# Decode attention beside a SwiGLU on one core: value products of 8 tokens by 64 columns, with two heads in one softmax chain

## The chip, the cores and the metric

The kernel runs on one core of one Trainium2 chip. The time is the device time of one execution in microseconds (us). TensorE is called PE in the profile's lines, VectorE DVE, ScalarE ACT, GpSimd POOL and SyncE SP; all bulk loads are issued from SP's queue and carried by the core's 16 DMA engines.

## The reference

One decode step for 4 sequences (B = 4, one query each). The input row x (640 wide) is normalised; from it come a sliding-window attention over cached keys and values and a SwiGLU, and both are added to x.

```python
x = A_x                                   # 4 x 1 x 640, bf16
xn = _layernorm(x, axis=-1)
q = (xn @ wq)                             # 32 heads of 192
k = k_cache[:, :, Sk - W:, :]             # Sk = 8192, W = 2048, 32 heads of 192
v = v_cache[:, :, Sk - W:, :]
p = _softmax(einsum(q, k) * 192 ** -0.5)
attn = einsum(p, v) @ wo                  # wo: 6144 x 640
h = _silu(xn @ w1) * (xn @ w3)            # 1536 wide
return x + attn + h @ w2
```

The keys and values that are read are 32 heads x 4 sequences x 2048 tokens x 192 numbers in bf16, twice: 201 MB. The weights wq, wo, w1, w3 and w2 add 22 MB. Every sequence has its own cache, so a key or a value is used once.

## The kernel before

**Layout.** The window of one head lies in a tile of 128 partitions: a partition holds 64 tokens (NJ) of one sequence, 12288 bf16 numbers, and partition number modulo 4 is the sequence. `load_k` (L98) and `load_v` (L103) each bring one head, 3072 KB, into one of three buffers (KBUFS, VBUFS). `wq` comes first, through the three V buffers; then three K.

**Scores.** A head is cut into 4 chunks of 16 tokens (CH = 16, NC = 4). `mult` (L216) multiplies a chunk of K by the query, which `q_bcast` (L207) has spread over the partitions for two heads at a time: 3072 products a partition on DVE. `adder` (L225) adds them up to 32 numbers a token: six products with the identity, accumulated in PSUM, each of 512 columns. `reduce_tile` (L233) adds those 32 on DVE. `RLAG` makes each reduction stand behind the multiply of two chunks later.

**Softmax chain, one per head.** `chain_lmax` takes the maximum per partition (DVE), `chain_tr` turns it to a row (PE), `chain_gmax` takes the maximum per sequence and spreads it (DVE), `chain_bc` brings it back to the partitions (PE), adds a bias that is -30000 for the three sequences that a partition does not hold (DVE, `negm`), and takes four exponentials, one for each sequence, on ACT (L270). So the weights z come out with three of four columns zero; an ACT instruction also leaves the row sum. `rowsum` (L274) adds these sums over the partitions and takes the reciprocal.

**Value products.** `pv` (L281) multiplies 2 tokens a partition at a time: z gives 32 columns of weights, of which 8 are used, and V 384 columns. Four such products run in the four strips of 32 columns of PE (`g = jj % NG`). 32 products make a head; ACT copies the 128 x 384 result to `o_sb` (L293). `fold` (L297) adds up the strips and the two tokens with two products with `rowsel`, and DVE scales the 4 x 192 result by the reciprocal (L306) into `o_bf`.

**Output.** For each group of four heads `ge_tr` (L308) transposes `o_bf`, and `ge_proj` (L315) multiplies it with that group's part of `wo`, loaded by `wo_load` (L108), into one accumulator for all groups. At the end `ffn_load`, `w2_load`, `ffn_mm` and `ffn_transpose` do the SwiGLU; the last products, with w2 (L420), wait for the last loads. L423 adds the parts and two small DMAs write the result.

**Order.** A table `sched` of slots is written by `add(slot, phase, fn, ...)`: a slot is one chunk, and within a slot the phase orders the calls. The functions are called in that order, and each engine runs its instructions in its own order. Tiles come from pools; a load waits until the last reader of its buffer is done. SP's order of loads is K, V, K, V with `wo` between; towards the end it is K of head 31, V of heads 29 and 30, w1, V of head 31, w3, the last wo and w2 in four pieces.

Of the kernel before, what the change touches and what calls it, by code (L numbers as in the profile page):

```python
# [10 lines left out]
FP32 = mybir.dt.float32  # L11
# [7 lines left out]
def kernel(  # L19
# [12 lines left out]
    DD: int = 32,  # L32
    CH: int = 16,
    HG: int = 4,
    QP: int = 2,
    KBUFS: int = 3,
    VBUFS: int = 3,
    PBUFS: int = 4,
    NZ: int = 3,
    L: int = 9,  # L40
    RLAG: int = 2,
    ALIGN: int = 128,
):

# [16 lines left out]
    NS = H * NC  # L61
    RPP = (HG * Dh) // P
    QW = QP * Dh
    OW = HG * Dh
    NCH = 512
    FC = F // P
    DH = D // 2
    assert NJ % CH == 0 and CH * DD <= 512 and QW <= 512 and CH % 2 == 0
    assert (HG * Dh) % P == 0 and Dh % RPP == 0 and H % HG == 0 and HG % QP == 0
# [3 lines left out]
    NB = H // QP // NG  # L73
    assert H % (QP * NG) == 0 and NB <= 4
    assert DH <= 512 and F % NCH == 0 and NF <= NG and (NJ // 2) % NG == 0 and 2 * B <= 32

# [9 lines left out]
    ps_o = ctx.enter_context(tc.tile_pool(name="ps_o", bufs=2, space=MemoryType.PSUM))  # L86
# [4 lines left out]
    qbcs, wos, o_pss, rss, rcps, o_sbs, o_bfs, chs = ({} for _ in range(8))  # L91
    mult_insts = {}
# [5 lines left out]
    def load_k(h):  # L98
        kt = kpool.tile([P, NJ, Dh], BF16, tag="kt")
        nc.sync.dma_start(out=kt[:], in_=cache_rows(A_k_cache, h))  # L100
        kts[h] = kt

    def load_v(h):  # L103
        vt = vpool.tile([P, NJ, Dh], BF16, tag="vt")
        nc.sync.dma_start(out=vt[:], in_=cache_rows(A_v_cache, h))
        vts[h] = vt
# [6 lines left out]
    x_sb = const.tile([B, D], BF16, name="x_sb")  # L113
# [24 lines left out]
    ones_f = const.tile([P, 1 + ALIGN // 4], FP32, name="ones_f")[:, 0:1]  # L138
    nc.vector.memset(ones_f[:], 1.0)
    nsc = const.tile([1, B], FP32, name="nsc")  # L140
    nc.vector.memset(nsc[:], -SCALE)

    zs = []
    for i in range(NZ):
        z = const.tile([P, NJ // 2, 32], BF16, name=f"z{i}")
        nc.gpsimd.memset(z[:], 0.0)
        zs.append(z)
# [5 lines left out]
    rowsel = const.tile([P, 2 * B], FP32, name="rowsel")  # L153
    nc.vector.tensor_reduce(out=rowsel[:], in_=idf[:].rearrange("p (g c) -> p c g", g=NG)[:, 0:2 * B, :], axis=AX.X, op=ALU.add)
# [9 lines left out]
    sq = ppool.tile([B, D], FP32, tag="pr")  # L164
    ssq = const.tile([B, 1], FP32, name="ssq")
    nc.scalar.activation(out=sq[:], in_=xc[:], func=ACTF.Square, accum_out=ssq[:])
# [6 lines left out]
    xn = const.tile([B, D], BF16, name="xn")  # L173
# [10 lines left out]
    nc.vector.tensor_copy(out=sel[:], in_=rowsel[:, 0:B].unsqueeze(1).to_broadcast([P, NQ, B]))  # L184
    selT = ps_t.tile([P, B], FP32, tag="t")
    nc.tensor.matmul(selT[:], lhsT=sel[0:B].rearrange("k q b -> k (q b)"), rhs=idb[0:B, 0:B], start=True, stop=True)
    mbias = const.tile([P, B], FP32, name="mbias")
    nc.vector.tensor_scalar(out=mbias[:], in0=selT[:], scalar1=-1.0, scalar2=-MASK, op0=ALU.add, op1=ALU.mult)
# [4 lines left out]
    for k in range(NB):  # L193
        pool, tag = ((ps_add, "ps"), (ps_o, "o_ps"))[k // 2]
        qp = pool.tile([P, QW], FP32, tag=tag)
        q_pss.append(qp)
# [7 lines left out]
    for k in range(NB):  # L204
        nc.scalar.copy(out=q_sb[:, k, :], in_=q_pss[k][:])

    def q_bcast(qg):  # L207
        k, g = qg // NG, qg % NG
        bp = ps_t.tile([P, QW], FP32, tag="t")
        nc.tensor.matmul(bp[:], lhsT=sel[32 * g:32 * g + B].rearrange("k q b -> k (q b)"),  # L210
                         rhs=q_sb[32 * g:32 * g + B, k, :], start=True, stop=True)
        qbc = qpool.tile([P, QP, Dh], BF16, tag="qbc")
        nc.scalar.copy(out=qbc[:].rearrange("p h d -> p (h d)"), in_=bp[:])  # L213
        qbcs[qg] = qbc

    def mult(s):  # L216
        h, c = s // NC, s % NC
        pr = ppool.tile([P, CH, Dh], BF16, tag="pr")
        mi = nc.vector.tensor_tensor(out=pr[:], in0=kts[h][:, c * CH:(c + 1) * CH, :],  # L219
                                     in1=qbcs[h // QP][:, h % QP, :].unsqueeze(1).to_broadcast([P, CH, Dh]),  # L220
                                     op=ALU.mult)
        prs[s] = pr
        mult_insts[s] = mi
# [8 lines left out]

    def reduce_tile(s):  # L233
        h, c = s // NC, s % NC
        if c == 0:
            sc = small.tile([P, NJ], FP32, tag="sc", bufs=3)
            scs[h] = sc
        ri = nc.vector.tensor_reduce(out=scs[h][:, c * CH:(c + 1) * CH], in_=pss.pop(s)[:], axis=AX.X, op=ALU.add)  # L238
        ahead = min(s + RLAG, NS - 1)
        if ahead in mult_insts and ahead > s:  # L240
            tc.add_manual_dep(ri.ins, mult_insts[ahead].ins.name, ORDER_DEP, reason="vector engine issue order")

    def chain_lmax(h):
        lmax = small.tile([P, 1], FP32, tag="lmax")
        nc.vector.tensor_reduce(out=lmax[:], in_=scs[h][:], axis=AX.X, op=ALU.max)  # L245
        chs[h] = [lmax]

    def chain_tr(h):
        mt = ps_t.tile([P, P + B], FP32, tag="t")
        nc.tensor.transpose(out=mt[0:1, 0:P], in_=chs[h][0][:], identity=idf[:])  # L250
        chs[h].append(mt)

    def chain_gmax(h):
        gmax = small.tile([1, B], FP32, tag="gmax")
        nc.vector.tensor_reduce(out=gmax[:], in_=chs[h][1][0:1, 0:P].rearrange("o (q b) -> o b q", b=B),
                                axis=AX.X, op=ALU.max)
        gmq = small.tile([1, NQ, B], FP32, tag="gmq", bufs=1)
        nc.vector.tensor_copy(out=gmq[:], in_=gmax[:].unsqueeze(1).to_broadcast([1, NQ, B]))  # L258
        chs[h].append(gmq)

    def chain_bc(h):
        lmax, mt, gmq = chs.pop(h)
        sc = scs.pop(h)
        nc.tensor.matmul(mt[:, P:P + B], lhsT=gmq[:].rearrange("o q b -> o (q b)"), rhs=nsc[:], start=True, stop=True)  # L264
        negm = small.tile([P, B], FP32, tag="negm")
        nc.vector.tensor_tensor(out=negm[:], in0=mt[:, P:P + B], in1=mbias[:], op=ALU.add)  # L266
        z = zs[h % NZ][:].rearrange("p j (s b) -> p j s b", b=B)
        rs = small.tile([P, B], FP32, tag="rs")
        for b in range(B):
            nc.scalar.activation(out=z[:, :, 0:2, b], in_=sc[:].rearrange("p (j s) -> p j s", s=2), func=ACTF.Exp,  # L270
                                 bias=negm[:, b:b + 1], scale=SCALE, accum_out=rs[:, b:b + 1])
        rss[h] = rs

    def rowsum(h):  # L274
        tb = ps_t.tile([B, 1], FP32, tag="t")
        nc.tensor.matmul(tb[:], lhsT=rss.pop(h)[:], rhs=ones_f[:], start=True, stop=True)  # L276
        rcp = small.tile([B, 1], FP32, tag="rcp")
        nc.vector.reciprocal(out=rcp[:], in_=tb[:])  # L278
        rcps[h] = rcp

    def pv(s):  # L281
        h, c = s // NC, s % NC
        if c == 0:
            o_ps = ps_o.tile([P, 2 * Dh], FP32, tag="o_ps")
            o_pss[h] = o_ps
        o_ps, z, vt = o_pss[h], zs[h % NZ], vts[h]
        for jj in range(c * CH // 2, (c + 1) * CH // 2):
            g = jj % NG
            nc.tensor.matmul(o_ps[32 * g:32 * g + 32, :], lhsT=z[:, jj, :], rhs=vt[:, 2 * jj:2 * jj + 2, :],  # L289
                             start=(jj < NG), stop=(jj >= NJ // 2 - NG))  # L290
        if c == NC - 1:
            o_sb = opool.tile([P, 2, Dh], FP32, tag="o_sb")
            nc.scalar.copy(out=o_sb[:].rearrange("r two d -> r (two d)"), in_=o_pss.pop(h)[:])  # L293
            o_sbs[h] = o_sb
            vts.pop(h)

    def fold(h):  # L297
        hg, hl = h // HG, h % HG
        fp = ps_t.tile([B, Dh], FP32, tag="t")
        o_sb = o_sbs.pop(h)  # L300
        for two in range(2):
            nc.tensor.matmul(fp[:], lhsT=rowsel[:, two * B:(two + 1) * B], rhs=o_sb[:, two, :], start=(two == 0), stop=(two == 1))  # L302
        if hl == 0:
            o_bf = opool.tile([B, HG, Dh], BF16, tag="o_bf")
            o_bfs[hg] = o_bf
        nc.vector.tensor_scalar_mul(out=o_bfs[hg][:, hl, :], in0=fp[:], scalar1=rcps.pop(h)[:, 0:1])  # L306

    def ge_tr(hg):  # L308
# [4 lines left out]
        nc.vector.tensor_copy(out=oTs[hg % 2][:, :, 0:B], in_=gp[:])  # L313

    def ge_proj(hg, i):  # L315
        oT = oTs[hg % 2]
        wo_t = wos[hg]
        st = (hg == 0 and i == 0)
# [48 lines left out]
    for h in range(H):  # L367
        s0 = h * NC
        if h >= KBUFS:
            add(s0 - (KBUFS - 1) * NC, 0, load_k, h)  # L370
# [86 lines left out]
```

## Time and profile before

| | |
|---|---|
| median of 3 runs | 529.87 us |
| lowest and highest run | 528.54 and 530.36 us |
| the profiled execution: time, span | 528.51 us, 526.6 us |
| mean granted clock of TensorE | 0.853 |
| busy: PE, DVE, ACT, POOL | 360.0, 340.2, 76.4, 4.5 us |
| moved by the DMA engines | 223.33 MB, mean 424 GB/s |

The span runs from the first to the last instruction of the profiled execution, and 1.9 us of its time lie outside it. Busy times are sums over instructions; a profile cuts the span in 40 slices of 13.2 us and gives, for each, tenths of busy time by engine and the rate of the DMA engines. "Issue to landing" of a load is the time from its DMA instruction on SP to its completion, with the time that it stands behind others.

### The profile page before, as it was taken

Reading aid. Unit: us, or ns where it says so; the run is one execution under the profiler, and the core shown is the slowest. Engines: PE = TensorE matmul, PEld = TensorE weight load, DVE = VectorE, ACT = ScalarE, POOL = GpSimd, SP = SyncE. Lnnn points to the kernel's source line nnn. Section 1 sums busy time; section 2 is a strip of 40 time slices with the busy share of each in tenths; the row PEclk is TensorE's granted clock in tenths of the full one; section 3 lists DMA queues with packets and bytes.
Section 4 is the critical chain, followed back from the end, with each engine's and each line's share of the span. In section 5 each row is a group of like instructions: output and inputs, shape, how many; then the busy total and the mean of one; then the engine's idle time right before and its main releaser. Section 6 shows DMA issues by size and latency. Waiting matters only on the chain.

```text
span 526.6 us, 5872 instructions
## 1 busy us (share of the span) xinstructions
PE 360.0 (68%) x2384; PEld 148.4 (28%) x2384; DVE 340.2 (65%) x475; ACT 76.4 (15%) x318; POOL 4.5 (1%) x14
## 2 busy tenths in 40 slices
PE   1356767886676778767567976767678766668755
PEld 1122222332222333232222322223233322223322
DVE  4069766677666557777556677666567775665802
ACT  2101211101111111101111011111111011111130
POOL 3000000000000000000000000000000000000000
PEclk9999988778788887887878787888887887888888
DMA  8999999999999999999999999999999999999995
GB/s 359 439 425 437 429 429 431 432 424 435 437 429 435 429 434 429 433 432 431 429 433 428 426 440 426 437 429 431 432 433 431 429 436 430 431 426 440 423 426 218
DMA packets 11730, 223.33 MB, mean 424 GB/s; under 512 B 1316, under 2 KB 1464, under 8 KB 2872
## 3 DMA queue, kind: packets, MB, share of 16 engines
q1 hardware_dynamic: 11688, 222.97, 98.7%
q8 instruction: 18, 0.29, 0.2%
q14 instruction: 8, 0.07, 0.0%
q10 hardware_dynamic: 16, 0.01, 0.0%
HBM read 222.96 MB, written 0.01 MB: 423 GB/s over the span
## 4 chain that ended last, share of the span: by engine, by line
DMA 66%; DVE 21%; PE 9%; ACT 2%; issue 2%; SPq 0%; DVEq 0%; ACTq 0%
DMA kt<-in_A_k_cache_dram 61%; DVE pr L219 15%; PE ps L229 6%; DMA w2t<-in_B_w_dram 5%; DVE sc L238 5%; PE o_ps L289 1%; ACT z L270 1%; PE acc L321 1%; ACT o_sb L293 0%; DVE lmax L245 0%; SPq L129 0%; PE gp L312 0%; PE tb L276 0%; DVE rcp L278 0%; SPq L335 0%
## 5 line engine op out<-in xcount | busy, mean ns | idle before, releaser
L229 PE MATMUL ps<-pr,idb 128*128 128x512 bf16 x768 | 241.0, 470 | 110.4 <-DVE sc L238 101.1
L219 DVE TENSOR_TENSOR pr<-kt,qbc 128x3072 bf16<-128x3072 bf16 x128 | 223.3, 1745 | 35.5 <-DMA kt<-in_A_k_cache_dram 35.4
L229 PEld LDWEIGHTS <-idb 128*128 128x128 bf16 x768 | 85.3, 115 | 240.0 <-issue 190.4
L238 DVE TENSOR_REDUCE sc<-ps 128x16 f32<-128x512 f32 x128 | 86.9, 679 | 0.9 <-PE ps L229 0.9
L293 ACT COPY o_sb<-o_ps 128x384 f32<-128x384 f32 x32 | 15.1, 472 | 306.5 <-PE o_ps L289 306.5
L289 PE MATMUL o_ps<-vt,z 128*32 128x384 bf16 x1024 | 55.3, 334 | 3.8 <-DMA vt<-in_A_v_cache_dram 3.8
L270 ACT ACTIVATE z<-sc,negm 128x64 bf16<-128x64 f32 x128 | 45.7, 423 | 76.7 <-DVE negm L266 76.7
L266 DVE TENSOR_TENSOR negm<-mt,mbias 128x4 f32<-128x4 f32 x32 | 5.2, 161 | 70.7 <-PE mt L264 70.7
L306 DVE TENSOR_SCALAR o_bf<-fp,rcp 4x192 bf16<-4x192 f32 x32 | 12.9, 405 | 56.8 <-PE fp L302 29.9
L302 PE MATMUL fp<-o_sb,rowsel 128*4 128x192 f32 x128 | 26.7, 332 | 13.2 <-ACT o_sb L293 13.2
L289 PEld LDWEIGHTS <-z 128*32 128x32 bf16 x1024 | 25.0, 97 | 29.4 <-issue 20.8
L270 ACT ACTIVATION_READ_ACCUMULATOR z<-sc,negm 128x1 f32 x128 | 23.9, 187 | 0.0
L302 PEld LDWEIGHTS fp<-o_sb,rowsel 128*4 128x4 f32 x128 | 8.7, 87 | 24.2 <-ACT o_sb L293 18.6
L276 PE MATMUL tb<-ones_f,rs 128*4 128x1 f32 x64 | 6.2, 166 | 13.4 <-ACT z L270 13.4
L264 PE MATMUL mt<-nsc,gmq 1*128 1x4 f32 x64 | 12.2, 258 | 1.2 <-DVE gmq L258 1.2
L264 PEld LDWEIGHTS mt<-nsc,gmq 1*128 1x128 f32 x64 | 9.4, 183 | 12.1 <-issue 10.3
L276 PEld LDWEIGHTS tb<-ones_f,rs 128*4 128x4 f32 x64 | 3.6, 86 | 24.5 <-ACT z L270 23.0
L278 DVE RECIPROCAL rcp<-tb 4x1 f32<-4x1 f32 x32 | 4.9, 153 | 8.5 <-PE tb L276 8.5
L201 PE MATMUL qp<-wt,xnT 128*32 128x384 bf16 x80 | 7.0, 523 | 4.9 <-DMA wt<-in_A_wq_dram 4.9
L250 PE MATMUL mt<-idf,lmax 128*1 128x128 f32 x32 | 9.9, 308 | 0.5 <-DVE lmax L245 0.4
L321 PE MATMUL acc<-wt,oT 128*32 128x320 bf16 x96 | 9.7, 301 | 0.3 <-DVE oT L313 0.2
L213 ACT CAST qbc<-bp 128x384 bf16<-128x384 f32 x16 | 7.6, 485 | 7.7 <-PE bp L210 7.7
(61 smaller groups left out, 80.1 us busy)
## 6 DMA issues: line engine op xcount, KB each, us to landing
kt<-in_A_k_cache_dram SPq DMA_DIRECT2D x32, 3072.0 KB, 36.8
vt<-in_A_v_cache_dram SPq DMA_DIRECT2D x32, 3072.0 KB, 40.1
wt<-in_A_wo_dram SPq DMA_DIRECT2D x8, 960.0 KB, 36.5
wt<-in_A_wq_dram SPq DMA_DIRECT2D x2, 3072.0 KB, 13.2
wt<-in_B_w_dram SPq DMA_DIRECT2D x2, 1920.0 KB, 32.5
wt<-in_A_wq_dram SPq DMA_DIRECT2D x1, 1536.0 KB
w2t<-in_B_w_dram SPq DMA_DIRECT2D x2, 640.0 KB, 26.9
w2t<-in_B_w_dram SPq DMA_DIRECT2D x1, 480.0 KB, 27.6
```

The costliest lines, as they stand in the source:

```text
L219: mi = nc.vector.tensor_tensor(out=pr[:], in0=kts[h][:, c * CH:(c + 1) * CH, :], in1=qbcs[h // QP][:, h % QP, :].unsqueeze(1).to_broadcast ...
L229: nc.tensor.matmul(ps[:], lhsT=idb[:], rhs=pr[:, :, kk * DD:(kk + 1) * DD], start=(kk == 0), stop=(kk == NK - 1))
L238: ri = nc.vector.tensor_reduce(out=scs[h][:, c * CH:(c + 1) * CH], in_=pss.pop(s)[:], axis=AX.X, op=ALU.add)
L250: nc.tensor.transpose(out=mt[0:1, 0:P], in_=chs[h][0][:], identity=idf[:])
L264: nc.tensor.matmul(mt[:, P:P + B], lhsT=gmq[:].rearrange("o q b -> o (q b)"), rhs=nsc[:], start=True, stop=True)
L270: nc.scalar.activation(out=z[:, :, 0:2, b], in_=sc[:].rearrange("p (j s) -> p j s", s=2), func=ACTF.Exp, bias=negm[:, b:b + 1], scale=SCAL ...
L276: nc.tensor.matmul(tb[:], lhsT=rss.pop(h)[:], rhs=ones_f[:], start=True, stop=True)
L289: nc.tensor.matmul(o_ps[32 * g:32 * g + 32, :], lhsT=z[:, jj, :], rhs=vt[:, 2 * jj:2 * jj + 2, :], start=(jj < NG), stop=(jj >= NJ // 2 - NG))
L293: nc.scalar.copy(out=o_sb[:].rearrange("r two d -> r (two d)"), in_=o_pss.pop(h)[:])
L302: nc.tensor.matmul(fp[:], lhsT=rowsel[:, two * B:(two + 1) * B], rhs=o_sb[:, two, :], start=(two == 0), stop=(two == 1))
L306: nc.vector.tensor_scalar_mul(out=o_bfs[hg][:, hl, :], in0=fp[:], scalar1=rcps.pop(h)[:, 0:1])
L321: nc.tensor.matmul(acc[32 * t:32 * t + 32, :], lhsT=oT[:, i, :], rhs=wo_t[:, i * D + t * DH:i * D + (t + 1) * DH], start=st, stop=sp)
```

## The change

The kernel is cut in other pieces; the loads and the sums stay the same.

- The chunk doubles: CH = 32, NC = 2. `mult` handles 6144 products, `adder` takes twelve products that leave 16 numbers a token (DD = 16), and `reduce_tile` adds those. There are two `pr` buffers of twice the size for four. Queries are spread for eight heads at a time, in three pieces of 512 columns.
- Two heads (HH = 2, a pair u) share one softmax chain: one maximum step, one transpose, one `negm`, one reciprocal for both. The exponential is taken once for each head, without the bias, and `chain_z` multiplies it on DVE by a mask `selb` that is one for the partition's own sequence: z for both heads at once.
- `pv` takes 8 tokens and 64 columns of the head at a time: 32 columns of weights, all used, and 512 columns of V; the three thirds of the head's 192 columns run in three strips. 24 products make a head, in one slot. Only the part of the result where weight and value are of the same token counts: `pick` multiplies by a mask `diag`, `pick_sum` adds over the tokens, both on DVE and both for two heads at once, except in the last pair, where each head has its own. `fold` brings the strips together for two heads, and the scaling by the reciprocal goes to ACT (L344 after).
- Small DVE steps are tied behind the multiply of the slot in which they are called (`behind`), one chunk later than what they use.
- There is one PSUM buffer `o_ps` of two heads for two of one head. Some tiles share buffers, and the masks are made from the identity at the start.

The diff, cut to its core:

```diff
-    DD: int = 32,
-    CH: int = 16,
+    DD: int = 16,
+    CH: int = 32,
     HG: int = 4,
-    QP: int = 2,
+    QP: int = 8,
     KBUFS: int = 3,
     VBUFS: int = 3,
-    PBUFS: int = 4,
-    NZ: int = 3,
-    L: int = 9,
-    RLAG: int = 2,
-    ALIGN: int = 128,
+    PBUFS: int = 2,
+    L: int = 7,
+    ALIGN: int = 144,
...
+    slot = [0]
+
+    def behind(inst):
+        if slot[0] in mult_insts:
+            tc.add_manual_dep(inst.ins, mult_insts[slot[0]].ins.name, ORDER_DEP, reason="vector engine issue order")
+
     def reduce_tile(s):
...
-        ahead = min(s + RLAG, NS - 1)
-        if ahead in mult_insts and ahead > s:
-            tc.add_manual_dep(ri.ins, mult_insts[ahead].ins.name, ORDER_DEP, reason="vector engine issue order")
+        behind(ri)
...
-        for b in range(B):
-            nc.scalar.activation(out=z[:, :, 0:2, b], in_=sc[:].rearrange("p (j s) -> p j s", s=2), func=ACTF.Exp,
-                                 bias=negm[:, b:b + 1], scale=SCALE, accum_out=rs[:, b:b + 1])
+        for hh in range(HH):
+            nc.scalar.activation(out=e[:, hh, :], in_=sc[:, hh, :], func=ACTF.Exp,
+                                 bias=negm[:, hh:hh + 1], scale=SCALE, accum_out=rs[:, hh:hh + 1])
...
+    def chain_z(u):
+        e = es.pop(u)
+        z = small.tile([P, HH, NJ, B], BF16, tag="z", bufs=2)
+        behind(nc.vector.tensor_tensor(out=z[:].rearrange("p h j b -> p (h j) b"),
+                                in0=e[:].rearrange("p h j -> p (h j)").unsqueeze(2).to_broadcast([P, HH * NJ, B]),
+                                in1=selb[:].unsqueeze(1).to_broadcast([P, HH * NJ, B]), op=ALU.mult))
+        zts[u] = z
...
-        for jj in range(c * CH // 2, (c + 1) * CH // 2):
-            g = jj % NG
-            nc.tensor.matmul(o_ps[32 * g:32 * g + 32, :], lhsT=z[:, jj, :], rhs=vt[:, 2 * jj:2 * jj + 2, :],
-                             start=(jj < NG), stop=(jj >= NJ // 2 - NG))
-        if c == NC - 1:
-            o_sb = opool.tile([P, 2, Dh], FP32, tag="o_sb")
-            nc.scalar.copy(out=o_sb[:].rearrange("r two d -> r (two d)"), in_=o_pss.pop(h)[:])
...
+        GN = NJ // PL
+        for g in range(GN):
+            for k in range(NV):
+                nc.tensor.matmul(o_ps[32 * k:32 * k + 32, hh, :],
+                                 lhsT=z[:, hh, g * PL:(g + 1) * PL, :].rearrange("p l b -> p (l b)"),
+                                 rhs=vt[:, g * PL:(g + 1) * PL, k * DV:(k + 1) * DV],
+                                 start=(g == 0), stop=(g == GN - 1))
+
+    def pick(u, h0, h1):
...
+        n = (h1 - h0) * PL
+        behind(nc.vector.tensor_tensor(out=o_ms[u][:, h0:h1].rearrange("r h l d -> r (h l) d"),
+                                       in0=o_pss[u][0:NV * 32, h0:h1, :].rearrange("r h (l d) -> r (h l) d", l=PL),
+                                       in1=diag[0:NV * 32, h0:h1, :].rearrange("r h l -> r (h l)").unsqueeze(2).to_broadcast([NV * 32, n, DV]), op=ALU.mult))
+
+    def pick_sum(u, h0, h1):
...
+        behind(nc.vector.tensor_reduce(out=o_rs[u][:, h0:h1, :], in_=o_ms[u][:, h0:h1].rearrange("r h l d -> r h d l"), axis=AX.X, op=ALU.add))
...
-        for two in range(2):
-            nc.tensor.matmul(fp[:], lhsT=rowsel[:, two * B:(two + 1) * B], rhs=o_sb[:, two, :], start=(two == 0), stop=(two == 1))
...
-        nc.vector.tensor_scalar_mul(out=o_bfs[hg][:, hl, :], in0=fp[:], scalar1=rcps.pop(h)[:, 0:1])
+        for k in range(NV):
+            nc.tensor.matmul(fp[:, :, k * DV:(k + 1) * DV], lhsT=fsel[0:NV * 32, k, :], rhs=o_r[:], start=True, stop=True)
...
+        for hh in range(HH):
+            nc.scalar.mul(out=o_bfs[hg][:, pr + hh, :], in_=fp[:, hh, :], mul=rcp[:, hh:hh + 1])
...
+    PS = HH * NC
+    for j in range(H):
+        if j >= KBUFS:
+            add(NC * j - 3, 0, load_k, j)
+        add(NC * j + 2, 8, load_v, j)
+        add(NC * j + L, 2, pv, j)
+    for s in range(NS):
+        add(s, 1, mult, s)
+        add(s, 3, adder, s)
+        add(s + 1, 4, reduce_tile, s)
+    for u in range(H // HH):
+        e = u * PS + PS - 1
+        add(e + 1, 5, chain_lmax, u)
+        add(e + 2, 2, chain_tr, u)
+        add(e + 2, 5, chain_gmax, u)
+        add(e + 3, 2, chain_bc, u)
+        add(e + 3, 5, chain_z, u)
+        add(e + 4, 2, rowsum, u)
...
+        add(PS * u + NC + L + 3, 2, fold, u)
...
-    add(end + L - NC, 0, ffn_mm, 1)
-    add(end + L + 1, 7, ffn_mm, 3)
-    add(end + L + 3, 7, ffn_transpose)
+    add(end + 4, 0, ffn_mm, 1)
+    add(end + 9, 0, ffn_mm, 3)
+    add(end + 10, 0, ffn_transpose)
```

## The prediction

> **What bounds the kernel now.** I read the page first: the span, the slices of the DMA engines, the queues.
>
> ```profile
> span 526.6 us, 5872 instructions
> ...
> DMA  8999999999999999999999999999999999999995
> GB/s 359 439 425 437 429 429 431 432 424 435 437 429 435 429 434 429 433 432 431 429 433 428 426 440 426 437 429 431 432 433 431 429 436 430 431 426 440 423 426 218
> ...
> q1 hardware_dynamic: 11688, 222.97, 98.7%
> q8 instruction: 18, 0.29, 0.2%
> ```
>
> The 16 DMA engines are busy in every slice but the first and the last, and 38 slices in a row move 423 to 440 GB/s. A slice is 13.17 us; the 223.33 MB less the 359 and 218 GB/s of the two end slices make 215.7 MB in 500.3 us, 431 GB/s. No compute engine comes near: PE 68%, DVE 65%, ACT 15%. So the span is the start, the stream of 223 MB, and what follows the last byte. The chain on the page names vector and matrix steps for a third of the span, but only because the issue of a K load waits for a multiply to free its buffer. Whether that issue is early or late is told by the answers for the tiles `kt` and `vt`:
>
> ```profile
> L100 SPq DMA_DIRECT2D kt<-in_A_k_cache_dram x32: 534/535/674, 2.1 to 449.1; - x32
> ...
> DMA to landing us min/median/max: 34.8/36.8/41.3
> ```
>
> ```profile
> L105 SPq DMA_DIRECT2D vt<-in_A_v_cache_dram x32: 534/535/596, 13.8 to 483.2; - x32
> ...
> DMA to landing us min/median/max: 29.8/40.1/43.2
> ```
>
> One load is 3.146 MB, 7.3 us at 431 GB/s. It lands 37 to 40 us after its issue, so four others stand ahead of it and some 30 us of compute delay are free in every head. Third, the end, by windows of 1 us (PEclk is the figure after PE to POOL, then the DMA share and GB/s):
>
> ```profile
> 510.00:511.00 1.00, 0.00 (x0) 0.00 (x0) 0.00 (x0) 0.00 (x0) 0.00 (x0) 1.00 1.08 464
> ...
> 513.00:514.00 1.00, 1.00 (x19) 0.55 (x12) 0.00 (x0) 0.00 (x0) 0.00 (x0) 0.50 1.01 428
> ...
> 516.00:517.00 1.00, 0.50 (x10) 0.47 (x12) 0.43 (x2) 0.00 (x0) 0.00 (x0) 1.00 1.05 437
> ...
> 520.00:521.00 1.00, 1.00 (x17) 0.67 (x13) 0.43 (x2) 0.00 (x0) 0.00 (x0) 1.00 0.56 229
> ...
> 522.00:523.00 1.00, 0.56 (x10) 0.29 (x6) 0.00 (x0) 0.00 (x0) 0.00 (x0) 1.00 0.10 40
> ```
>
> The stream thins out from 519 us: some of the 16 engines finish up to 4 us before the slowest. And fourth, the timeline from the landing of the last V:
>
> ```profile
> 511.86 2.75 PE L289 MATMUL o_ps<-vt,z 128*32 128x384 bf16 x32 [3.81 <-DMA vt<-in_A_v_cache_dram]
> ...
> 514.65 0.48 ACT L293 COPY o_sb<-o_ps 128x384 f32<-128x384 f32 x1 [5.32 <-PE o_ps L289]
> ...
> 515.19 0.81 PE L302 MATMUL fp<-o_sb,rowsel 128*4 128x192 f32 x4 [0.58 <-ACT o_sb L293]
> ...
> 516.87 1.26 PE L342 MATMUL gt<-wt,xnT 128*32 128x512 bf16 x15
> ...
> 518.79 0.42 DVE L353 TENSOR_TENSOR hb<-sg,t_bf 96x512 bf16<-96x512 bf16 x1 [1.64 <-ACT t_bf L346]
> ...
> 519.55 0.99 PE L321 MATMUL acc<-wt,oT 128*32 128x320 bf16 x12
> ...
> 520.38 0.71 PE L420 MATMUL ff<-w2t,hT 128*32 128x320 bf16 x8
> 521.75 0.72 PE L420 MATMUL ff<-w2t,hT 128*32 128x320 bf16 x8 [0.66 <-DMA w2t<-in_B_w_dram]
> 522.91 0.72 PE L420 MATMUL ff<-w2t,hT 128*32 128x320 bf16 x8 [0.44 <-DMA w2t<-in_B_w_dram]
> 523.67 0.48 DVE L423 TENSOR_TENSOR res<-ff,t 64x320 bf16<-64x320 f32 x1 [2.25 <-PE ff L420]
> ```
>
> The last eight products of w2 wait for data until 522.91; everything before them waits less. That is the wait that ends last. The attention tail has a small margin to it.
>
> **The change, part by part.** *The stream.* Same loads, sizes, queue and three buffers each. On SP only a wo load changes places with a neighbouring K or V load, which costs nothing as long as all are issued early. Engine traffic does not slow the stream: 428 GB/s between 30 and 60 us with DVE 91% busy, 427 between 480 and 500 with 64%. Cost 0.
>
> *The lead of the loads.* DVE's small steps now stand behind a multiply that waits for K, and the values of a head are multiplied in the second half-chunk slot three heads later, so V buffers come free later. Let K of head j land at T; heads follow at 2 x 7.3 = 14.6 us. Two multiplies: I price one of 6144 elements from L219 (1745 ns for 3072) and L353 (422 ns for 512), which give 0.517 ns an element: 3.34 us (at most 2 x 1.745 = 3.49). PE sums 24 products a head as before, some 1.4 us for six (the chain's `PE ps` rows), 2.9 us a chunk. With the mask multiply and the value products ahead of the second chunk, V's buffer of head j-3 or j-2 is free 9 to 11 us after a K landing, and queued behind it on SP is a K load. The issue of a V then falls from 40 us ahead of its landing to about 51 - 25 = 26 us (four heads' K and V between them); K goes from 37 to about 33. A V needs 7.3. Cost 0, covered by some 18 us in each head; were that cover gone, each us missing would be paid up to 29 times.
>
> *DVE, for two heads.* Out: 8 multiplies x 1.745 + 8 reductions x 0.679 + 2 x (0.208 + 0.269 + 0.214 + 0.161 + 0.153 + 0.405) = 22.2 us. In: 4 x 3.34 + 4 x 0.68 + one chain of five steps, 1.1 + the mask multiply z + `pick` and `pick_sum` on 1024 f32 elements. L423 (320 f32 from PSUM, 483 ns) and L238 (512, 679 ns) give 1.02 ns an element, so 1.20 each. z is 512 bf16: 0.42 by L353, 0.68 by L238; its first operand is repeated with step 0, which no row shows, so I take 0.68. Sum 20.2 us: DVE falls by about 2 us in every 29.2, some 32 us of 340, all beside the stream: worth 0. The Trainium skill ("VectorE: DVE Perf Modes", section "Mode 2×_1P") asks step 1 of every 16-bit operand for the double rate, which speaks against z; by it z keeps the dearer price, which no row here shows, and the sum stays.
>
> *PE and ACT.* Value products: 32 of 384 columns in four strips become 24 of 512 in three, 8 rounds of 512 columns for 8 of 384, a third longer: about +0.6 us a head. ACT loses six of eight exponentials a pair with their accumulator reads (0.423 + 0.187) and two copies (0.472), and gains two scalings. All hidden; PE is idle for 5 us in a head (32% of the span over 32 heads).
>
> *The start.* DVE builds more masks and three query broadcasts precede the first multiply instead of two; ACT's six copies of 384 columns at 0.49 become six of 512 at 0.58 (L346's 512), +0.6 us, while the first K lands only at 30.3. Cost 0.
>
> *The tail.* From 511.86, where V of the last head lands, in after's order on PE: value products, fold, w3's products, transposes, output projection, w2's products. Value products: three strips, like L342, whose five rounds of 512 took 2.19 us at a granted 0.50 (504.59) and 1.26 at 1.00 (516.87). Eight rounds are 3.50 or 2.02; the clock there is 0.50, so they end at 515.4 (before: 514.6). `pick` and `pick_sum` on 512 elements, 0.68 + 0.05 to pass the semaphore, twice: 516.85. Fold: 3 x 128 columns for two heads is what 2 x 192 were, 0.81: 517.7. ACT scales two heads, 0.8 (two of the 0.42 us row): 518.5. Beside that PE runs w3's products, 1.26: 519.0; cast 0.58, product 0.42, transposes 0.36 and gaps: 520.5, and only then, in PE's order, the projection, 0.99: 521.5. Three eights of w2 at 0.72: 523.66, against 522.91 + 0.74 = 523.65 before. So the margin is used up exactly; cost 0.0. If the value products got the full clock it is -1.5 us of slack and still 0; if the two new DVE steps and two scalings each cost 0.2 more, +0.8; if PE is granted half again after its gap, more (first rival).
>
> *Instruction words.* Fewer instructions on PE: 3696 rows in its order for 4322. The 18 fetches (16 KB each) should become about 15 or 16. Spread over all DMA engines two or three less are worth 0.1 us; on the slowest engine alone, at 431/16 = 27 GB/s, 0.6 us each, 1.8. I take 0.1.
>
> Sum: 526.6 - 0.1 + 0.1 (half a chance of a late tail) = 526.6 us of span, 528.5 with the 1.9 around it (528.51 for that execution). The median of the runs, 529.87, lies 1.4 above that execution; I forecast 529.8.
>
> **The rivals.** *Slower, the clock in the tail (and a tail longer than counted).* The change puts 1.45 us of DVE between the value products and the fold, on a PE that had 0.50 from 512 to 515 after idling from 509. If half is granted from about 518, the projection and w2's products take 1.74 times as long (2.19/1.26): 0.74 x (0.99 + 2.16) = +2.3 us, 532.2. It decides as soon as the projection ends after 521.5. The Trainium skill ("TensorE: Matmul & The Clock Gate", section "Part 1: The HAM clock gate") holds that only an idle window of about 3.4 us brings half the clock; the idle 508.6 to 511.8 before the 0.50 fits, and by it the gap of 1.45 us would cost nothing. Chance 0.16, with the same end reached by dearer steps.
>
> *Slower, the queue runs dry.* V issues come later than 29 us after the landing they follow. At 1 us a head that is +29, 559 us. Against it stands the 18 us of cover. 0.04.
>
> *Faster, the slowest DMA engine has less to do.* The thinning from 519 to 523 is 16 engines ending apart; three fetches less on the last of them take 1.8 us, 528.0 by the median. For it: everything after V's landing shifts along. Against: nothing shows which engine carries the fetches. 0.13.
>
> *No change that can be told,* the forecast: 0.67.
>
> **How the numbers follow.** A measurement of this kernel tells about 0.3%, 1.6 us, from no change. Likeliest 529.8; the fetches at their bound give 528.0, the tail at half the clock 532.2, and the runs before spread by 0.9 around their middle. Range 527.9 to 532.1, outside it the dry queue and the outermost of both ends. Faster 0.13, same 0.67, slower 0.20.
>
> **What would show it.** Right: DMA still 9 in all middle slices near 431 GB/s; V landing 24 to 29 us after issue and K 31 to 35; DVE near 308 us, a multiply at 3.34, z at 0.4 to 0.7, `pick` of both heads at 1.2; the last products of w2 still waiting for DMA, or starting within 0.3 us of it; the projection ending near 1.4 us before the last w2 byte. Wrong: a slice under 420 GB/s in the middle (dry queue), the last chain running V, `pick`, fold, projection without a DMA wait behind it (tail), or a stream that ends over 1.5 us earlier (fetches).

## The result, and the profile after

| after | |
|---|---|
| median of 6 runs | 526.94 us (526.79 to 527.74) |
| median of 6 runs of before beside it | 529.61 us (528.51 to 531.14) |
| the profiled execution: time, span | 526.79 us, 525.0 us |
| mean granted clock of TensorE | 0.844 |
| busy: PE, DVE, ACT, POOL | 326.4, 328.3, 39.6, 1.8 us |

After takes 0.9955 of the time of before, with a 95% interval of 0.9936 to 0.9974. Of the 2.7 us between the medians, 1.7 (0.3%) are in the two profiled executions. The rest depends on which runs of before are in the comparison: its 101 runs in the four later comparisons fall in two groups, 72 between 528.05 and 529.1 us and 29 from 529.2 to 531.4, and four of the six here lie in the upper one. After's six runs and the 22 of e4, f1 and e5 below, which are after with small edits, lie closer: 22 of the 28 between 526.79 and 527.16, six between 527.6 and 527.91. In the later comparisons, where before's median is 528.4 to 528.6, the gain is about 1.5 us.

The stream did not change. The page of after, with the slices of the DMA engines and the queues:

```profile
span 525.0 us, 4658 instructions
...
GB/s 360 433 436 428 431 436 426 438 426 433 431 432 432 433 434 427 436 429 429 439 424 434 429 435 426 438 422 439 434 430 429 430 434 434 430 433 430 426 428 256
...
q1 hardware_dynamic: 11688, 222.97, 99.0%
q8 instruction: 15, 0.25, 0.2%
```

Every slice between the first and the last still moves 422 to 439 GB/s, and q1 carries the same packets and bytes. What is smaller is q8, the instruction words: 15 fetches for 18. The answers for the tiles `kt` and `vt` of after, a load's issue and its time to landing:

```profile
L107 SPq DMA_DIRECT2D kt<-in_A_k_cache_dram x32: 534/550/687, 2.1 to 447.4; - x32
...
DMA to landing us min/median/max: 30.7/34.3/41.1
```

```profile
L112 SPq DMA_DIRECT2D vt<-in_A_v_cache_dram x32: 534/535/595, 13.4 to 493.6; - x32
...
DMA to landing us min/median/max: 25.6/32.4/38.4
```

A V load now lands 32.4 us after its issue, 40.1 before, and one load needs 7.3 us: the lead is still four loads deep. The page's costliest groups (busy us, mean ns of one, idle time before them and its releaser) hold the vector engine's terms (the 17 of L331 and of L323 are 15 for two heads, 1912 and 1209 ns each, and two for one head):

```profile
L228 DVE TENSOR_TENSOR pr<-kt,qbc 128x6144 bf16<-128x6144 bf16 x64 | 214.5, 3352 | 166.8 <-DMA kt<-in_A_k_cache_dram 166.8
...
L331 DVE TENSOR_REDUCE o_r<-o_m 96x128 f32<-96x1024 f32 (+1 forms) x17 | 30.7, 1807 | 0.1
...
L323 DVE TENSOR_TENSOR o_m<-o_ps,diag 96x1024 f32<-96x1024 f32 (+1 forms) x17 | 19.5, 1148 | 7.6 <-PE o_ps L313 7.6
...
L291 DVE TENSOR_TENSOR z<-e,selb 128x512 bf16<-128x512 bf16 x16 | 10.8, 678 | 0.9 <-ACT e L283 0.9
```

DVE now waits 166.8 us for K: it is not the bound. Then the end, the timeline from the landing of the last V (start, length, what; in brackets the wait before it):

```profile
510.43 1.91 PE L313 MATMUL o_ps<-vt,z 128*32 128x512 bf16 x24 [0.62 <-DMA vt<-in_A_v_cache_dram]
...
512.39 0.69 DVE L323 TENSOR_TENSOR o_m<-o_ps,diag 96x512 f32<-96x512 f32 x1 [2.51 <-PE o_ps L313]
513.11 1.01 DVE L331 TENSOR_REDUCE o_r<-o_m 96x64 f32<-96x512 f32 x1
...
517.57 0.99 PE L357 MATMUL acc<-wt,oT 128*32 128x320 bf16 x12
...
518.63 0.72 PE L467 MATMUL ft<-w2t,hT 128*32 128x320 bf16 x8
...
520.17 0.72 PE L467 MATMUL ft<-w2t,hT 128*32 128x320 bf16 x8 [0.81 <-DMA w2t<-in_B_w_dram]
...
521.31 0.72 PE L467 MATMUL ft<-w2t,hT 128*32 128x320 bf16 x8 [0.42 <-DMA w2t<-in_B_w_dram]
...
522.07 0.48 DVE L470 TENSOR_TENSOR res<-ft,attn_bf 64x320 bf16<-64x320 f32 x1 [2.63 <-PE ft L467]
```

The same wait ends last, the last eight products of w2 for their load, but at 521.31 instead of 522.91: 1.60 us, the whole difference of the spans. The last V, too, landed 1.43 us sooner (510.43 for 511.86). So the stream itself ended earlier, at the same rate and with the same bytes. The windows of 1 us of after show what is missing (PEclk after POOL, then DMA share and GB/s):

```profile
521.00:522.00 1.00, 0.69 (x8) 0.41 (x7) 0.00 (x0) 0.00 (x0) 0.00 (x0) 1.00 0.13 47
522.00:523.00 1.00, 0.03 (x2) 0.00 (x0) 0.48 (x1) 0.00 (x0) 0.00 (x0) 1.00 0.00 0
```

In before the DMA engines still had a share of 0.10 between 522 and 523: in the trace's packet records two of the 16 engines end there, at 522.8 and 523.0, while six end near 521.3, one at 521.87 and the other seven sooner. In after the latest seven end between 521.1 and 521.4, and nobody behind them.

### The profile page after: what moved, and what is told of

Same layout as the page of the kernel before. It is cut to its first block, busy times and chain, and to the rows that moved or that the text cites. A ratio compares the mean times of both kernels' runs of the same rounds, so it can differ in the third digit from the quotient of the medians.

```text
span 525.0 us, 4658 instructions
## 1 busy us (share of the span) xinstructions
PE 326.4 (62%) x1991; PEld 142.2 (27%) x1991; DVE 328.3 (63%) x289; ACT 39.6 (8%) x121; POOL 1.8 (0%) x11
## 4 chain that ended last, share of the span: by engine, by line
DMA 77%; DVE 13%; PE 8%; SPq 1%; issue 0%; DVEq 0%
DMA kt<-in_A_k_cache_dram 73%; DVE pr L228 11%; PE ps L238 6%; DMA w2t<-in_B_w_dram 5%; PE o_ps L313 1%; DVE sc L253 1%; SPq L112 0%; DVE o_r L331 0%; SPq L136 0%; DVE o_m L323 0%; PE acc L357 0%; SPq L372 0%; PE ft L467 0%; DVE z L291 0%; DVE res L470 0%
## 5 line engine op out<-in xcount | busy, mean ns | idle before, releaser
L238 PE MATMUL ps<-pr,idb 128*128 128x512 bf16 x768 | 223.7, 452 | 166.3 <-DVE pr L228 166.3
L228 DVE TENSOR_TENSOR pr<-kt,qbc 128x6144 bf16<-128x6144 bf16 x64 | 214.5, 3352 | 166.8 <-DMA kt<-in_A_k_cache_dram 166.8
L313 PE MATMUL o_ps<-vt,z 128*32 128x512 bf16 x768 | 66.3, 389 | 1.2 <-DMA vt<-in_A_v_cache_dram 0.6
L253 DVE TENSOR_REDUCE sc<-ps 128x32 f32<-128x512 f32 x64 | 43.7, 683 | 6.8 <-PE ps L238 6.7
L331 DVE TENSOR_REDUCE o_r<-o_m 96x128 f32<-96x1024 f32 (+1 forms) x17 | 30.7, 1807 | 0.1
L283 ACT ACTIVATE e<-sc,negm 128x64 bf16<-128x64 f32 x32 | 10.9, 340 | 239.4 <-DVE negm L279 239.4
L323 DVE TENSOR_TENSOR o_m<-o_ps,diag 96x1024 f32<-96x1024 f32 (+1 forms) x17 | 19.5, 1148 | 7.6 <-PE o_ps L313 7.6
L344 ACT ACTIVATE o_bf<-fp,rcp 4x192 bf16<-4x192 f32 x32 | 11.4, 403 | 132.0 <-PE fp L338 132.0
L338 PE MATMUL fp<-o_r,fsel 96*4 96x128 f32 x96 | 13.1, 273 | 1.8 <-DVE o_r L331 1.8
L291 DVE TENSOR_TENSOR z<-e,selb 128x512 bf16<-128x512 bf16 x16 | 10.8, 678 | 0.9 <-ACT e L283 0.9
## 6 DMA issues: line engine op xcount, KB each, us to landing
kt<-in_A_k_cache_dram SPq DMA_DIRECT2D x32, 3072.0 KB, 34.3
vt<-in_A_v_cache_dram SPq DMA_DIRECT2D x32, 3072.0 KB, 32.4
```

The lines of the kernel that those rows point to most:

```text
L228: mi = nc.vector.tensor_tensor(out=pr[:], in0=kts[j][:, c * CH:(c + 1) * CH, :], in1=qbcs[j // QP][:, j % QP, :].unsqueeze(1).to_broadcast ...
L238: nc.tensor.matmul(ps[:], lhsT=idb[:], rhs=pr[:, :, kk * DD:(kk + 1) * DD], start=(kk == 0), stop=(kk == NK - 1))
L253: ri = nc.vector.tensor_reduce(out=scs[j // HH][:, j % HH, c * CH:(c + 1) * CH], in_=pss.pop(s)[:], axis=AX.X, op=ALU.add)
L283: nc.scalar.activation(out=e[:, hh, :], in_=sc[:, hh, :], func=ACTF.Exp, bias=negm[:, hh:hh + 1], scale=SCALE, accum_out=rs[:, hh:hh + 1])
L291: behind(nc.vector.tensor_tensor(out=z[:].rearrange("p h j b -> p (h j) b"), in0=e[:].rearrange("p h j -> p (h j)").unsqueeze(2).to_broadc ...
L313: nc.tensor.matmul(o_ps[32 * k:32 * k + 32, hh, :], lhsT=z[:, hh, g * PL:(g + 1) * PL, :].rearrange("p l b -> p (l b)"), rhs=vt[:, g * PL: ...
```

## Experiments

The theory: the two late engines of before are those that carried one more of q8's fetches, so the time goes by how many instructions PE has. The main rival: other buffer addresses, or something else in the new order, sped up the stream. In all tables *fetches* are q8's, *V31* is the start in us of the last head's value products, which begin when V lands, and the ratio is to the runs of before beside it.

**Instructions put back.** The kernel after, with n tiny products in every slot, into columns of `acc`'s bank that nothing reads (e1 six, e2 sixteen, f1 two, f2 four, f3 twenty), 128 instructions for each step of n:

```diff
+    def extra(n):
+        for _ in range(n):
+            nc.tensor.matmul(acc_full[64:96, 320:324], lhsT=idb[:, 0:32], rhs=idb[:, 0:4], start=True, stop=True)
...
+        add(s, 3, extra, 6)
```

e1: 

> The changed kernel with 6 more tiny products (32 columns of weights, 4 of data, into a part of PSUM that nobody reads) in each of the 64 slots: 768 more PE instructions, 4464 rows in PE's order for 3696, nothing else changed. Fetch theory (the end is set by the slowest DMA engine, which also carries PE's instruction words): 18 fetches of 16 KB as in the kernel before, and the time goes back up by 0.6 us (fetches spread over several engines) to 1.8 us (three on the slowest, 16 KB at 27 GB/s each): 527.6 to 528.8. Rival (the gain comes from the order of the loads, the place of the buffers or the tail): 526.9, no change, since PE has over 2 us free in a slot of 7.3.

e2: 

> As the run with 6 more tiny products, with 16 in each slot: 2048 more PE instructions, 5744 rows, some 8 more fetches than the changed kernel, 23 in all. Fetch theory: 3 times the shift of the smaller dose, +1.6 to +4.9 us, 528.5 to 531.8. Rival: 526.9; at most a little more if the 1.2 us of PE time in each slot were to reach the path.

f1: 

> The changed kernel with 2 more tiny PE products in each slot: 256 instructions, 3952 rows, 16 fetches. Staircase theory (PE's fetches go round in turn over 8 of the 16 DMA engines, each costs its engine about 1.4 us, and the engine with the most sets the end, so the time goes by the number of fetches over 8, rounded up: 15 and 16 give 2, 17 to 24 give 3): 526.9, as the changed kernel. Proportional theory (each fetch adds its share): +0.3 to +0.6, 527.2 to 527.5.

f2: 

> The same with 4 in each slot: 512 instructions, 4208 rows, 17 fetches. Staircase theory: one engine now has a third, 528.3 to 528.4 as with 18 and with 23; of the last microsecond of the stream, 522 to 523, about one engine in 16 is busy. Proportional theory: 527.4 to 527.9.

f3: 

> The same with 20 in each slot: 2560 instructions, 6256 rows, 25 fetches. Staircase theory: a fourth on one engine, 1.4 us over the runs with 18 and 23, 529.8. Saturation theory (something else holds the end at 528.4, and the tiny products only bring that back): 528.4.

**Sums left out.** Fewer instructions, in before and in after, by ending `adder`'s loop early: e3 is before with 3 of 6 sums, g1 before with 4 of 6, e5 after with 6 of 12.

```diff
-        for kk in range(NK):
+        for kk in range(NK // 2):
...
-                             start=(kk == 0), stop=(kk == NK - 1))
+                             start=(kk == 0), stop=(kk == NK // 2 - 1))
```

e3: 

> The kernel before with three of the six sums of a chunk left out (the scores are those of half the head's width, so the output is another): 768 PE instructions fewer, 3554 rows for 4322, 15 fetches for 18; every load, the order and the place of the buffers and DVE's work stay. Fetch theory: faster than the kernel before by as much as the change is, 527.0 (by 0.6 to 1.8 us at least). Rival (order, place or tail of the changed kernel): 529.6, no change.

e5: 

> The changed kernel with six of the twelve sums of a chunk left out (scores of half the head's width, so the output is another): 768 PE instructions fewer, 2928 rows, 12 fetches for 15. Staircase theory: still 2 on the fullest engine, 526.9, and some of the seven engines that end last now end earlier; proportional theory: 525.4 to 526.5. If PE, less busy, is granted half its clock at the end, the tail adds up to 2 us to either, which the timeline shows as last products that wait for no load.

g1: 

> The kernel before with two of the six sums of a chunk left out (scores of two thirds of the head's width, so the output is another): 512 PE instructions fewer, 3810 rows for 4322, 16 fetches for 18, everything else as it was. Staircase theory: no engine has a third fetch, and the old kernel runs at 527.0, as the changed one; the window 522 to 523 shows no transfer. Rival (the change's other parts are needed too): 528.5, as before. If PE, less busy, is granted half its clock at the end, the tail hides part of it, as where half of the sums were left out.

**As few as possible.** g3 is after with 2 of 12 sums and 5 of 8 steps of the value products, and ten filler products ahead of the tail.

g3: 

> The changed kernel with ten of the twelve sums and three of every eight steps of the value products left out (the output is another), and ten filler products near the end that keep PE at work: 1860 rows, 8 fetches. Staircase theory: one fetch on each engine, 1.4 us under the changed kernel, 525.5, the lowest step but one; the stream's last microsecond is 519 to 520. Saturation theory (15 fetches and fewer no longer matter): 526.9. A PE at half its clock would add up to 2 us, which the timeline shows as last products without a wait for a load.

| kernel | fetches | V31 | median us (range) | ratio (95%) |
|---|---|---|---|---|
| g3 | 8 | 509.06 | 526.43 (525.65 to 527.96) | 0.9948 (0.9929 to 0.9967) |
| e5 | 12 | 510.46 | 527.06 (526.92 to 527.70) | 0.9974 (0.9963 to 0.9985) |
| after | 15 | 510.43 | 526.94 (526.79 to 527.74) | 0.9955 (0.9936 to 0.9974) |
| e3 | 15 | 510.77 | 528.26 (527.37 to 530.41) | 0.9999 (0.9984 to 1.0013) |
| f1 | 16 | 510.90 | 527.03 (526.89 to 527.91) | 0.9967 (0.9951 to 0.9983) |
| g1 | 16 | 510.77 | 527.98 (527.16 to 529.99) | 0.9985 (0.9970 to 1.0000) |
| f2 | 17 | 512.08 | 528.27 (527.95 to 529.22) | 0.9991 (0.9979 to 1.0003) |
| e1 | 18 | 512.06 | 528.41 (528.10 to 529.08) | 0.9994 (0.9985 to 1.0003) |
| before | 18 | 511.86 | 528.4 to 528.6 in four comparisons | 1 |
| e2 | 23 | 511.77 | 528.45 (528.34 to 529.23) | 0.9995 (0.9983 to 1.0006) |
| f3 | 25 | 513.04 | 529.61 (529.38 to 530.53) | 1.0014 (1.0004 to 1.0025) |

The column V31 is a staircase: 509.1 with 8 fetches, 510.4 to 510.9 with 12 to 16, 511.8 to 512.1 with 17 to 23, 513.0 with 25. Its steps lie between 8 and 12, at 16 to 17, and between 23 and 25; they are 1 to 1.4 us high. That is the form of fetches dealt in turn to eight engines: the fullest engine has one, two, three or four, and the last bytes of a load wait for the fullest. e2 first contradicted the theory as I had it: sixteen products a slot were to cost about three times what six cost, and cost the same. f1, f2 and f3 were then chosen to have the fetch counts 16, 17 and 25 at the edges of a staircase, and fell on it. The DMA share between 522 and 523 us counts the engines that have one more. The windows of e2 (23 fetches) and of f2 (17), then of f3 (25) one microsecond later:

```profile
522.00:523.00 1.00, 0.55 (x10) 0.30 (x6) 0.00 (x0) 0.00 (x0) 0.00 (x0) 1.00 0.34 129
```

```profile
522.00:523.00 1.00, 1.00 (x10) 0.57 (x8) 0.48 (x2) 0.00 (x0) 0.00 (x0) 0.50 0.07 26
```

```profile
523.00:524.00 1.00, 0.63 (x8) 0.35 (x8) 0.00 (x0) 0.00 (x0) 0.00 (x0) 1.00 0.06 24
```

0.34 of 16 engines is five or six busy throughout; in e2's packet records seven engines end between 522.7 and 523.0. 0.07 is one engine, and in f2 one ends at 523.0, the seventeenth fetch. 0.06 is again one, f3's twenty-fifth, at 524.1. So a single one of the 16 engines sets the time, and one fetch makes the step. In each of these runs as many engines end last as the fetches leave over when divided by eight: two in before (18 fetches), four in e5 (12), seven in after (15) and e2 (23), one in f2 and f3.

The packet records show the deal and the price of a fetch directly. The 18 fetches of before take, in order, 947, 879, 880, 934, 938, 925, 962, 962 ns, then 956, 884, 880, 935, 929, 922, 967, 962, then 954 and 879: a row of eight durations that comes round again, within 9 ns. And the 24 KB packet that begins as a fetch ends takes 1380 to 1462 ns in after, where most take 912. Fetch and lengthened packet together hold up the engine by 1.42 to 1.43 us, in 14 of after's 15 fetches; behind the last one comes no such packet. That is the step's height.

The runs of e3 and g1 show a second thing. Both end their stream with the lower step (V31 at 510.77, no DMA after 522), yet e3's median did not move. Each has two groups of runs: six of e3's twelve and six of g1's lie between 527.16 and 527.68, below all 101 runs of before (528.05 and more), and the others from 528.29 up. So half of the runs show the step, about 1 us; the 0.4 to 0.5 us that they still lie above after are not explained. The timelines of g1 and of e3:

```profile
521.90 0.72 PE L420 MATMUL ff<-w2t,hT 128*32 128x320 bf16 x8 [0.45 <-DMA w2t<-in_B_w_dram]
```

```profile
521.88 3.41 PE L420 MATMUL ff<-w2t,hT 128*32 128x320 bf16 x24
...
525.33 0.48 DVE L423 TENSOR_TENSOR res<-ff,t 64x320 bf16<-64x320 f32 x1 [2.37 <-PE ff L420]
```

In g1's profiled execution (527.36 us) the last eight wait for the load. In e3's (530.03 us, one of the longer of its runs) all 24 w2 products start only at 521.88, when the load is there, and take 3.41 us at a granted clock of 0.50 where three eights take 2.16 at 1.00: the tail has become the bound and gives back what the fetches gave. f2's profiled execution, 529.22 us and the longest of its runs, has the same: its stream ends at 523.0, but its 24 products take 3.03 us from 521.43 at 0.50. With 3 of 6 sums left out PE idles more (mean granted clock 0.668). g3 shows it too: its stream is earliest, but its 24 w2 products take 3.02 us from 518.51, at half the clock until 521, without a wait for DMA; only its best runs, 525.65 and 525.69, reach the next step down.

**Places of the buffers.** `ALIGN` is the size of an unused tile that moves the K and V buffers; with it they start at an odd multiple of 256 bytes in after, and at a multiple of 512 in before. e4 sets 400 for 144 (a multiple of 512 again), h3 sets 112 (32 bytes below a multiple of 256).

e4: 

> The changed kernel with ALIGN = 400 for 144, which shifts every later tile in SBUF by 256 bytes, so that the K, V and wo buffers start at multiples of 512 bytes as in the kernel before (in the changed one at odd multiples of 256). Place theory: the gain of 2.7 us goes, or part of it. Fetch theory: 526.9, no change.

e4: 526.95 us (526.79 to 527.66), ratio 0.9971 (0.9960 to 0.9982). Where the tiles lie modulo 512 does nothing, and f2 and e1, whose extra products leave the loads and the buffers where after has them, lose the gain: the rivals of the addresses and of the order are out for this change.

**Instructions on ACT.** g2 adds eight tiny copies a slot on ACT, 512 in all; h2 is g2 with `ALIGN` 112, because g2's small tile had also moved the buffers by 32 bytes.

g2: 

> The changed kernel with 8 tiny ACT copies (4 numbers a partition) behind each multiply: 512 more ACT instructions, four more fetches of 8 KB, PE as it is. If every engine's fetches go round the same eight DMA engines as PE's: one or two of them end 0.7 us later, 527.2 to 528.3. If ACT's fetches have an engine of their own, which ends at about 520.2 now and has 1.1 us to spare: up to four times 0.7 us on it, 526.9 to 528.6. If they cost nothing: 526.9. ACT has 40 us of work in 525, and 1.8 us more in each slot.

h2: 

> The run with 8 more tiny ACT copies in each slot again, with ALIGN = 112, so that the 32 bytes of its extra tile are taken back and the K and V buffers start at multiples of 256 bytes, as in all other runs. If ACT's own fetches (six more of 8 KB) cost that run its time: 531.2 again. If the place of the buffers did: 526.9 to 528.2, the upper end where one engine gets most of ACT's fetches.

h3: 

> The changed kernel with ALIGN = 112 for 144 alone: every later tile lies 32 bytes lower in SBUF, so the K, V and wo buffers start 32 bytes before a multiple of 256. If the place of a buffer within 256 bytes sets what a packet of 24 KB takes (915 to 922 ns for 912 in the run with ACT copies): +3.2 us, 530.1, all 16 engines later alike. If not: 526.9.

| kernel | buffers modulo 256 | q14 fetches | median us (range) | ratio (95%) |
|---|---|---|---|---|
| g2 | 32 | 10 | 531.16 (531.03 to 531.31) | 1.0041 (1.0028 to 1.0054) |
| h2 | 0 | 10 | 527.49 (527.04 to 527.76) | 0.9971 (0.9960 to 0.9983) |
| h3 | 224 | 4 | 530.51 (530.30 to 531.14) | 1.0035 (1.0023 to 1.0047) |

g2 alone would have read as a price of 4 us for ACT's instructions. h2 and h3 part the two: 512 instructions on ACT cost at most 0.6 us over after (527.49 for 526.94, in different comparisons), and a start of the buffers 32 bytes off costs 3.6 us with the same instructions as after (530.51). In h3's packet records a 24 KB packet takes 915 ns in the median, after's 912. The Trainium skill ("DMA: Bandwidth & Descriptors", section "How a descriptor splits into AXI transactions") has a descriptor that doesn't start at a multiple of 256 bytes need one transaction more; it speaks of reads, and here the side that is off is the one written. An estimate by that page is 97 for 96 in 24 KB, 1% of the stream. The 3.6 us measured are 0.7% of the span of 525 us, so the case agrees in kind.

**Which engines?** Two attempts to give the eight loaded engines less to do, by cutting one load into loads of 8 partitions: g4 the first w2 load in 16, h1 the w1 load in one of 96 and four of 8.

```diff
-        nc.sync.dma_start(out=ffn[2][:, n, c0:c1],
-                          in_=B_w2[n * NCH:(n + 1) * NCH, :].rearrange("(p c) n -> p c n", c=CF)[:, c0:c1])
+        w2r = B_w2[n * NCH:(n + 1) * NCH, :].rearrange("(p c) n -> p c n", c=CF)
+        step = 8 if n == 0 else P
+        for p0 in range(0, P, step):
+            nc.sync.dma_start(out=ffn[2][p0:p0 + step, n, c0:c1], in_=w2r[p0:p0 + step, c0:c1])
```

g4: 

> The changed kernel with the first of the four w2 loads issued as 16 loads of 8 partitions instead of one of 128, same bytes to the same place, nothing left out. If a load of 8 rows is carried by eight DMA engines, these move 40 KB more each and the other eight 40 KB less, 1.5 us at 27 GB/s. Should the first be the eight without PE's fetches, the fuller ones end 1.5 us earlier: 525.5, faster than both kernels. Should they be the ones with the fetches: 528.4. If the 16 loads spread over all engines: 526.9.

h1: 

> The changed kernel with the w1 load issued as one load of 96 partitions and four of 8, instead of one of 128; same bytes, nothing left out, five issues on SP for one. If a load of 8 rows is carried by eight DMA engines, these move two rows of 15 KB more and the others two less, 31 KB or 1.1 us at 27 GB/s. Should the eight be those without PE's fetches, the fuller ones end 1.1 us earlier: 525.8, faster than both kernels. Should they be the ones with fetches: 528.0. Half and half: 527.5 to 528.0.

g4: 532.34 us (532.20 to 532.68), ratio 1.0062 (1.0044 to 1.0081). h1: 538.81 us (537.19 to 539.18), ratio 1.0186 (1.0166 to 1.0207). Neither answers the question. In g4 the issue of 19 loads held SP for 26 us, where four took 3.3:

```profile
496.01 26.16 SPq L375 DMA_DIRECT2D w2t<-in_B_w_dram  x19
```

In h1 the engines are busy and move half as much; its window of 15 us from 495, which in after moves 430 GB/s:

```profile
495.00:510.00 15.00, 10.76 (x88) 5.23 (x86) 6.49 (x13) 1.49 (x6) 0.00 (x0) 0.77 1.02 207
```

Why, no run here tells.

## Why the prediction was wrong

The forecast was no change, 529.8 us, with a range from 527.9. The measured 526.94 is faster, and below the range.

- **Instruction words: the step that failed.** The count was right (15 or 16 fetches; 15), and the mechanism stood there as a rival at 0.13. The term was mis-sized: I took 0.1 us, all engines sharing the loss, with 1.8 as the other bound. The runs show the other end: one step of the staircase, 1.6 us in the profiled pair, because the fullest of the eight engines drops from three fetches to two. My case against it, that nothing shows which engine carries the fetches, was no reason for a small value: I had shown the 16 engines ending up to 4 us apart, and a load lands with its slowest engine. The engine-by-engine ends were in the trace before, and so was the price of a fetch. I had 0.6 us by its bytes; with the packet behind it, it is 1.43, so three of them on one engine would have been 4.3 us and not 1.8. That the gain came out at 1.6, near my bound, is luck: the fullest engine lost one fetch, not three.
- **The way from span to median.** I added the 1.4 us by which the median of three runs lay above the profiled execution. That median was from before's upper group. After's median is 0.15 us above its profiled execution, so 1.2 of the 2.9 us of error come from here, and the rival's 528.0 and the range's low end were too high by the same.
- **The stream: right.** No slice in the middle is below 422 GB/s, and the queue never ran dry.
- **The lead: right in kind.** K lands 34.3 us after issue (31 to 35 forecast); V 32.4, better than the 24 to 29.
- **DVE: wrong by 20 us, and worth nothing.** mult 3.35 (3.34), z 0.68 (0.68), `pick` 1.21 for two heads (1.20) are as costed. `pick_sum` is not: 1.91 us for two heads where I had 1.20, some 10 us in all. I took 1.02 ns an element from rows that read with step 1; it sums over the tokens, which lie 64 numbers apart in `o_m`; that the step is the cause was not tried by itself. The other 10 us come from adding up rows that overlap in time: DVE's rows of before add up to about 365 us for 340.2 us of busy time, those of after to about 344 for 328.3, so what went out was worth less than its rows. DVE went to 328.3 and not to 308. It is idle for 37% of the span, so the miss is hidden, but in a kernel bound by DVE it would have decided.
- **The tail: right that it costs nothing, wrong in its parts.** V's landing to the end of the projection took 8.1 us for 9.6. The value products had the full clock (1.91 us, not 3.50), since head 30's products and w1's keep PE busy until the last V comes (PE had waited 0.62 us for it, 3.81 in before); `pick_sum` took 1.01 for 0.73. The projection ends at 518.56, 2.7 us ahead of the last products of w2, where I had 1.4, just room for the two eights of w2 between.
- **The clock rival: not in after, but seen.** In after PE stood still for 1.8 us between the value products and the fold and kept a granted clock of 1.00. (The idle time ahead of before's 0.50, which I read as 508.6 to 511.8, was 3.81 us long, from 508.05.) Half the clock in the tail, as the slower rival had it, is what gave back e3's gain in the profiled run. It may also be what makes before's upper group, whose runs were not profiled; that is argued only, and the mean granted clock is 0.84 in both groups.

## What to carry to other kernels

When a kernel is bound by its stream of loads, as here, look at when each DMA engine ends, not at the mean share: the last load lands with the fullest engine, and a handful of instruction fetches can be what fills it. Then the number of instructions on an engine that is itself hidden has a price, paid in steps; leave room below a step rather than cut at random. And anchor a forecast on the profiled execution and the lowest group of runs, not on a median of three that may mix groups.

## What the runs showed of the hardware

- PE's instruction words come in fetches of 16 KB, and the time goes in steps of eight fetches, 1 to 1.4 us each. A fetch took 0.88 to 0.97 us, where 16 KB at 27 GB/s would be 0.6, and the 24 KB packet behind it 0.47 to 0.55 us more than the usual 0.91: 1.43 us in all. Which eight of the 16 engines carry them stays open.
- Load buffers 32 bytes off a multiple of 256 cost 3.6 us of 527 over the whole stream; 256 or 512 is the same.
- A DVE reduction over an axis whose numbers lie 64 f32 apart took 1.91 us for 1024 elements, 1.9 ns each; the reduction of 512 elements that lie in a row took 0.68 us, 1.3 ns each. The first reads what `pick` wrote in SBUF, the second PSUM, and the two differences were not parted.
- Sixteen loads of 8 partitions held the issuing queue for 26 us, and four of them (with one of 96) near the end of the stream halved its rate for 15 us.
